# Decode attention with a 512-key window: more wo rows on the lowest five DMA engines, an alignment directive for three instruction streams, and another order of the last sums

## The chip, the cores and the metric

The kernel runs on one core of one Trainium2 chip. The metric is the device time of one execution in microseconds (us). The time of before is the median of 3 runs. One further execution was profiled; its page and trace are what is read here.

## The reference

One token of 32 sequences attends to the last 512 keys of a cache. There are 32 query heads and 8 key and value heads of width 128; `W` is 512.

```python
q = (x @ wq).reshape(B, Sq, Hq, Dh).transpose(0, 2, 1, 3)        # 32 x 32 x 1 x 128
k = jnp.repeat(k_cache[:, :, Sk - W:, :], rep, axis=1)           # rep = 4
v = jnp.repeat(v_cache[:, :, Sk - W:, :], rep, axis=1)
scores = jnp.einsum("bhqd,bhkd->bhqk", q, k) * (Dh ** -0.5)
p = _softmax(scores, axis=-1)
o = jnp.einsum("bhqk,bhkd->bhqd", p, v)
return o.transpose(0, 2, 1, 3).reshape(B, Sq, Hq * Dh) @ wo      # wo: 4096 x 512
```

The inputs are bf16: `x` 32 x 512, `wq` 512 x 4096, `wo` 4096 x 512, and two caches of which 32 MB each are read. With `wq` and `wo` of 4 MB each that makes 75.5 MB.

## The kernel before

The batch is cut into eight groups `q` of four sequences. For each group the keys (4 MB) and the values (4 MB) are loaded into one of two buffers each, `K_sb[q % 2]` and `V_sb[q % 2]`, with 128 partitions of 32 KB. `wq` is loaded first, into `V_sb[1]`, and `wo` last, into `K_sb[0]`. The SyncE engine (SP) issues all of these loads in the order of the list `LOADS`: `K0 K1 V0.0 K2 V1.0 ... V7.0 V7.1 A0 A1 A2 A3 W0 W1 W2`. A load waits for the buffer it overwrites. ACT issues the three small loads of `x` at the very start.

What each engine does is written out by hand in the lists `PE_OPS`, `DVE_OPS` and `ACT_OPS`; the function `needs` gives the semaphores that an operation waits for. The letters, for a group q:

- `Tq.w`: DVE transposes half `w` of the keys from `K_sb` into `KT_sb[:, w]` (L491). `Sq.w`: the scores of that half on PE (L353). `M`: maximum (DVE). `X`: exponential (ACT). `N`: division by the sum (DVE).
- `E`: PE moves the probabilities into the layout of the values by 16 matmuls with selection matrices from `E_sb` (L368). `G`: ACT copies them from PSUM. `B`: DVE and ACT spread them into `bd` (L511, L552).
- `Pq.g0.g1`: probabilities times values on PE, 4 matmuls for each of 32 groups of rows (L383). `C`: DVE and ACT pick the diagonal blocks into `C_sb` (L516, L557).
- `F` and `H`: PE folds `C_sb` by head (L395) and the extra rows of each head (L404). `D` and `U`: ACT copies these into `o_sel` (L561) and `o_ext` (L566).

A head has 128 rows of `wo`. `NI` = 30: the first 4 x 30 rows lie on 4 partitions of `K_sb[0]`, 30 rows on each, loaded in three pieces `W0`, `W1`, `W2` of 20, 8 and 2 rows (`WOP`). The last `NX` = 8 rows of each head ("extra rows") lie on 32 partitions of `wx_row`, a view of `QT_sb[0:64]`, one head on each. They are loaded by `A0` to `A3` (L262), which `HEADS` cuts into 20, 5, 5 and 2 heads:

```python
HEADS = [(0, 20, 4, 0), (20, 25, 1, 32), (25, 30, 1, 33), (30, 32, 1, 34)]
```

`wx_row` is first set to zero by ACT (operation `Z0`, L572), since not all of its 64 partitions are written; `A0` waits for that.

The last sum into `Y_ps`, over heads and rows, goes as follows: PE waits for `D7`, then for W0 (80 matmuls, L421), then for `U7` and the extra rows (32 matmuls, L435), then for W1 (32) and W2 (8). The four quarters of the output columns lie on four groups of PSUM partitions; DVE (L524) and ACT (L582) each copy half, and SP and ACT store them.

POOL makes the selection matrices: `E_sb` holds, for each of 4 values of `k` and 4 of `e`, 128 columns that are zero but for every fourth (a memset, L297, and four copies, L301). It then builds the block diagonal queries `QBD` (L312) for each group. PE's instruction stream begins with `pe.addr_align(256, offset=178)` (L320), a directive that places the next instruction at slot 178 of a block of 256 instruction slots, here by no-ops.

Of the kernel before, what the change touches and what calls it, by code (L numbers as in the profile page):

```python
# [5 lines left out]
BF16 = mybir.dt.bfloat16  # L6
F32 = mybir.dt.float32
ACTF = mybir.ActivationFunctionType
# [10 lines left out]
PE_OPS = """  # L19
S0.0 S0.1 S1.0 S1.1 E0 E1 P0.0.32 S2.0 F0 H0 S2.1 P1.0.12 E2 P1.12.32 F1 H1 S3.0 S3.1 P2.0.12 E3  # L20
P2.12.32 F2 H2 S4.0 S4.1 P3.0.12 E4 P3.12.32 S5.0 S5.1 S6.0 P4.0.4 E5 P4.4.8 S6.1 P4.8.24 E6 P4.24.32
F3 H3 S7.0 P5.0.20 S7.1 P5.20.32 E7 F4 H4 P6.0.32 F5 H5 P7.0.32 F6 H6 F7 H7
"""
DVE_OPS = """
T0.0 T0.1 T1.0 M0 T1.1 N0 M1 N1 B0.0.4 B1.0.4 T2.0 T2.1 M2 N2 B2.0.4 T3.0 T3.1 M3 N3 B3.0.4 T4.0
# [2 lines left out]
"""  # L28
ACT_OPS = """
X0 X1 G0 B0.4.8 G1 B1.4.8 C0.0.4 D0 U0 X2 G2 B2.4.8 C1.0.4 D1 U1 X3 G3 B3.4.8 C2.0.4 D2 U2 X4 G4 B4.4.8  # L30
C3.0.2 X5 G5 B5.4.8 X6 G6 C4.0.2 B6.4.7 D3 U3 B6.7.8 Z0 X7 C5.0.2 G7 B7.5.6 D4 U4 B7.6.8 C6.0.2 D5 U5 C7.0.2
D6 U6 D7 U7
"""

LOADS = """
# [2 lines left out]

X_PARTS = [(0, 25), (25, 30), (30, 32)]
V_PIECES = 5 * [[0, 32]] + 2 * [[0, 16, 32]] + [[0, 18, 32]]  # L40
WOP = [(0, 20), (20, 28), (28, 30)]
HEADS = [(0, 20, 4, 0), (20, 25, 1, 32), (25, 30, 1, 33), (30, 32, 1, 34)]


# [4 lines left out]
def bass_standalone__sliding_block_cached__sampling_kernel(  # L49
# [8 lines left out]
    B, Sq, D = x.shape  # L58
    _, HKV, SK, DH = k_cache.shape
    HD = wq.shape[1]  # L60
    HQ = HD // DH
    REP = HQ // HKV
    W = min(4096, max(256, SK // 4))
    assert (B, Sq, D, HKV, SK, DH, HQ, REP, W) == (32, 1, 512, 8, 2048, 128, 32, 4, 512)
    P = 128
    DKT = D // P
    SCALE = float(DH) ** -0.5
    NQ = B // 4
    KB = 4
    R = W // KB  # L70
    NI = 30
    NX = DH - 4 * NI
    NG = 4

# [2 lines left out]
    ends, total = {}, {}  # L77
# [52 lines left out]
    with ExitStack() as es:  # L130
# [15 lines left out]
        o_sel = sb("o_sel", [P, NI, B], BF16)  # L146
        o_ext = sb("o_ext", [64, NX, B], BF16)
        F_ext = sb("F_ext", [P, 64], F32)
        E_sb = sb("E_sb", [P, KB, REP, 32, KB], BF16)
        F_sb = sb("F_sb", [P, 4, HQ, 4], F32)  # L150
        mask = sb("mask", [P, HKV], F32)
        maxv = sb("maxv", [P, NQ], F32)
# [4 lines left out]

        wq_sb = V_sb[1][:, :].rearrange("p (kt n) -> p kt n", kt=DKT)
        wo_sb = K_sb[0][:, 0:NI * D].rearrange("p (i n) -> p i n", i=NI)
        wx_row = QT_sb[0:64].rearrange("p j w h t -> p (j w h t)")  # L160
        wx_sb = wx_row.rearrange("p (i n) -> p i n", i=NX)


# [15 lines left out]
        def folds(q):  # L179
# [8 lines left out]
        sem_out = sem("sem_out")  # L188
        names = (
            "pe_xT pe_q pe_Y dve_xT dve_q dve_QT dve_m dve_r dve_c act_q act_warm out_y "  # L190
            "pool_x pool_e pool_ei pool_q pool_f pool_m pool_j pool_qbd pool_fz"
        ).split()
        s = {n: sem(n) for n in names}
        op_sem = {key: sem("op_%s_%s" % key) for key in total}
# [1 line left out]
        def v_waits(q, g0, g1):  # L196

            for i, g in enumerate(V_PIECES[q][:-1]):
                if g0 <= g < g1:
                    c = sum(1 for p in range(q % 2, q + 1, 2) if len(V_PIECES[p]) > i + 1)  # L200
                    yield g, sem_v[q % 2][i], 16 * c

        for b0, b1 in X_PARTS:
            nc.scalar.dma_start(
# [33 lines left out]
        @block.sync  # L238
        def _(sp):
            wait = Waits(sp)  # L240
            wo_h = wo.rearrange("(h r) n -> h (r n)", r=DH)
            wo_r = wo_h[:, 0:4 * NI * D].rearrange("h (d m) -> h d m", d=4)
            for op in ops_of(" ".join(LOADS)):
                kind, q = op[0], op[1]
                if kind == "K":
                    if q >= 2:
                        wait([ends["T", q - 2, 1]])
                    sp.dma_start(K_sb[q % 2][:, :], rows(k_cache, q)).then_inc(sem_k[q % 2], 16)
                elif kind == "V":
                    if q == 1:  # L250
                        sp.wait_ge(s["pe_q"], 8)
                    r0, r1 = (4 * g for g in V_PIECES[q][op[2]:op[2] + 2])
                    if q >= 2:
                        wait([ends["P", q - 2, r1 // 4 - 1]])
                    sp.dma_start(  # L255
                        V_sb[q % 2][:, r0 * DH:r1 * DH], rows(v_cache, q, r0, r1)
                    ).then_inc(sem_v[q % 2][op[2]], 16)
                elif kind == "A":
                    wait([ends["Z", 0]])
                    h0, h1, k, p0 = HEADS[q]  # L260
                    n = (h1 - h0) // k
                    sp.dma_start(  # L262
                        wx_row[p0:p0 + 4 * n:1 if k == 4 else 4, :],
                        wo_h[h0:h1, 4 * NI * D:].rearrange("(k j) m -> j k m", k=k),
                    ).then_inc(sem_wx, 16)
                else:
                    wait([ends["T", NQ - 2, 1]])
                    i0, i1 = WOP[q]
                    sp.dma_start(  # L269
                        wo_sb[:, i0:i1, :].rearrange("p i n -> p (i n)"),  # L270
                        wo_r[:, :, i0 * D:i1 * D],
                    ).then_inc(sem_wo[q], 16)
            store(sp, 0)

        @block.gpsimd
        def _(pool):
            wait = Waits(pool)

            def diag(t, pattern, name):
# [14 lines left out]

            diag(E_id[:, :, :].rearrange("p e (b h) -> p e b h", b=4),
                 [[-1, REP], [-4, 4], [-16, HKV]], "pool_ei")
            pool.memset(E_sb[:, :, :, :, :], 0.0).then_inc(s["pool_e"], 1)  # L297
            pool.wait_ge(s["pool_e"], 1)
            pool.wait_ge(s["pool_ei"], 2)
            for k in range(KB):  # L300
                pool.tensor_copy(E_sb[:, k, :, :, k], E_id[:, :, :]).then_inc(s["pool_e"], 1)  # L301
            pool.wait_ge(s["pool_e"], 5)
            pool.wait_ge(s["pool_q"], 1)
            pool.wait_ge(s["dve_QT"], 1)
            for q in range(NQ):
                if q >= 2:
                    wait([ends["S", q - 2, 1]])
                for b in range(4):
                    pr = slice(32 * b, 32 * b + 32)
                    if q or b:  # L310
                        pool.wait_ge(s["pool_qbd"], 4 * q + b)
                    pool.tensor_copy(  # L312
                        QBD[pr, q % 2].rearrange("p (w t) (h c) -> p w t h c", w=2, h=HKV)[
                            :, :, :, :, 4 * b:4 * b + 4],
                        QT_sb[pr, q].rearrange("p w (h e) t -> p w t h e", h=HKV),
                    ).then_inc(s["pool_qbd"], 1)

        @block.tensor
        def _(pe):
            pe.addr_align(256, offset=178)  # L320
            wait = Waits(pe)
            pe.wait_ge(s["pool_x"], 2)
            pe.wait_ge(sem_x, 16 * len(X_PARTS))
# [38 lines left out]

            def to_value_rows(q):
                if q == 0:
                    pe.wait_ge(s["pool_e"], 5)
                for e in range(REP):
                    for k in range(KB):
                        ins = pe.matmul(  # L368
                            EP_ps[:, e * R:(e + 1) * R],
                            lhsT=E_sb[:, k, e].rearrange("p m j -> p (m j)"),  # L370
                            rhs=P_bf[:, k * R:(k + 1) * R],
                            start=k == 0, stop=k == KB - 1, tile_position=(0, 0),
                        )
                return ins
# [35 lines left out]
            for op in orders["PE"]:  # L410
                wait(needs(op))
                run[op[0]](*op[1:]).then_inc(op_sem["PE", op[0]], 1)
            wait([ends["D", NQ - 1]])
            for j, (i0, i1) in enumerate(WOP):
                pe.wait_ge(sem_wo[j], 16)
                last = j == len(WOP) - 1
                for cs in ((0, 1), (2, 3)) if last else (range(4),):
                    for i in range(i0, i1):
                        for c in cs:
                            n = 2 * (c % 2) + c // 2  # L420
                            ins = pe.matmul(  # L421
                                Y_ps[32 * c:32 * (c + 1), 0:P],
                                lhsT=o_sel[:, i, :],
                                rhs=wo_sb[:, i, n * P:(n + 1) * P],
                                start=i == 0, stop=i == NI - 1, tile_position=(0, 32 * c),
                            )
                    if last:
                        ins.then_inc(s["pe_Y"], 1)
                if j == 0:
                    wait([ends["U", NQ - 1]])  # L430
                    pe.wait_ge(sem_wx, 16 * len(HEADS))
                    for i in range(NX):
                        for c in range(4):
                            n = 2 * (c % 2) + c // 2
                            pe.matmul(  # L435
                                Y_ps[32 * c:32 * (c + 1), 0:P],
                                lhsT=o_ext[:, i, :],
                                rhs=wx_sb[:, i, n * P:(n + 1) * P],
                                start=False, stop=False, tile_position=(0, 32 * c),
                            )  # L440

        def spread_args(q, h):
            return bd[:, q % 2, :, h, :], PTc[:, q % NG], mask[:, h:h + 1]
# [83 lines left out]
        def _(act):  # L527
# [39 lines left out]
                    o_ext[:, :, 4 * q:4 * q + 4],  # L567
                    EP_ps[0:64, 0:4 * NX].rearrange("p (b i) -> p i b", b=4), ACTF.Copy)

            def zero(_):  # L570
                act.wait_ge(s["pool_qbd"], 4 * NQ)
                return act.activation(  # L572
                    wx_row, junk[0:64, 0:1].to_broadcast([64, NX * D]), ACTF.Copy
                )

            run = {"X": exponential, "G": gather, "B": spread, "C": pick, "D": folded,
                   "U": folded_ext, "Z": zero}
            for op in orders["ACT"]:
                wait(needs(op))
                run[op[0]](*op[1:]).then_inc(op_sem["ACT", op[0]], 1)  # L580
# [34 lines left out]
```

## Time and profile before

| | us |
|---|---|
| median of 3 runs (lowest, highest) | 184.43 (184.24, 184.46) |
| profiled execution | 184.59 |
| its span | 183.3 |
| PE busy, share of the span | 120.4, 66% |
| DVE busy | 106.7, 58% |
| ACT busy | 54.2, 30% |
| POOL busy | 17.1, 9% |
| HBM read over the span | 75.53 MB, 412 GB/s |

The page divides the span into 40 slices and gives, for each, the busy tenths of an engine and the mean share of the 16 DMA engines. Its DMA part gives queues: q1 has the loads that SP issues, q10 the ones of ACT, and the queues of kind "instruction" (q8 and q14) fetch the engines' own instructions. The chain of waits follows the program back from its last instruction. The timeline lists instructions by start time, with the idle time before and what ended it.

### The profile page before, as it was taken

To read this page: it belongs to the slowest core of one execution; us is meant where nothing else is said; L and a number is where in the kernel's file an instruction comes from. 1 tells how busy PE (TensorE), PEld (TensorE's weight loads), DVE (VectorE), ACT (ScalarE), POOL (GpSimd) and SP (SyncE) were. 2 spreads that over 40 slices of the span, in tenths; PEclk is the share of its full clock that TensorE was granted. 3 is DMA by queue.
4 is the path that set the end of the run, shared out by engine and by line. 5 is a ranking of instruction groups with operands and counts; after the bars stand their busy time and mean duration, and the time that the engine had idled before them with its cause. 6 is when DMAs were issued, how large, how long until landed. Compare 5 with 4: busy or idle time off the path is not lost.

```text
span 183.3 us, 3870 instructions
## 1 busy us (share of the span) xinstructions
PE 120.4 (66%) x1676; PEld 58.0 (32%) x1676; DVE 106.7 (58%) x109; ACT 54.2 (30%) x101; POOL 17.1 (9%) x53
## 2 busy tenths in 40 slices
PE   0029802416779699429944995440799978999984
PEld 0013300002535344304520252000255433655463
DVE  0042399998569534973289326999825994703030
ACT  3001300010590527501650135001053693803040
POOL 7900013020200020002000200001000000000000
PEclk9999995555769999996995599655559999999999
DMA  6998999989999999999999999999999999999981
GB/s 234 459 443 386 429 458 454 422 386 451 458 443 383 429 454 447 415 401 451 442 429 415 424 442 440 408 429 451 436 408 404 426 426 429 432 418 427 436 359 62
DMA packets 3517, 75.80 MB, mean 414 GB/s; under 512 B 429, under 2 KB 525, under 8 KB 653
## 3 DMA queue, kind: packets, MB, share of 16 engines
q1 hardware_dynamic: 3409, 75.52, 96.5%
q8 instruction: 13, 0.21, 0.5%
q10 hardware_dynamic: 92, 0.05, 0.1%
q14 instruction: 3, 0.02, 0.0%
HBM read 75.53 MB, written 0.03 MB: 412 GB/s over the span
## 4 chain that ended last, share of the span: by engine, by line
DMA 65%; DVE 19%; PE 8%; issue 4%; SPq 3%; ACT 0%; DVEq 0%
DMA K_sb<-in_k_cache_dram 32%; DVE KT_sb L491 16%; DMA V_sb<-in_v_cache_dram 16%; DMA K_sb<-in_wo_dram 11%; DMA V_sb<-in_wq_dram 7%; PE ps L336 5%; PE ps L383 2%; DVE QT_sb L483 2%; SPq L262 2%; SPq L255 1%; PE ps L421 1%; PE ps L353 1%; DVE C_sb L516 0%; SPq L269 0%; ACT KT_sb L533 0%
## 5 line engine op out<-in xcount | busy, mean ns | idle before, releaser
L491 DVE STREAM_TRANSPOSE KT_sb<-K_sb 128x4096 f32<-128x4096 f32 x16 | 70.5, 4430 | 7.2 <-DMA K_sb<-in_k_cache_dram 7.1
L383 PE MATMUL ps<-V_sb,bd 32*128 32x512 bf16 x1024 | 64.0, 402 | 4.4 <-DMA V_sb<-in_v_cache_dram 2.1
L353 PE MATMUL ps<-KT_sb,QBD 128*32 128x512 bf16 x256 | 24.7, 522 | 35.2 <-DVE KT_sb L491 26.0
L383 PEld LDWEIGHTS ps<-V_sb,bd 32*128 32x128 bf16 x1024 | 27.7, 98 | 37.8 <-issue 14.1
L353 PEld LDWEIGHTS ps<-KT_sb,QBD 128*32 128x32 bf16 x256 | 6.4, 111 | 50.4 <-DVE KT_sb L491 31.3
L539 ACT ACTIVATE P_f<-ps,negmax 128x512 f32<-128x512 f32 x8 | 5.5, 687 | 56.8 <-DVE negmax L499 56.8
L557 ACT ACTIVATE C_sb<-ps 32x512 f32<-32x512 f32 x22 | 12.9, 588 | 24.4 <-PE ps L383 24.2
L552 ACT ACTIVATE bd<-PTc,mask 128x512 bf16<-128x512 bf16 x31 | 20.1, 712 | 0.3
L312 POOL COPY QBD<-QT_sb 32x128 bf16<-32x128 bf16 x32 | 9.3, 289 | 106.3 <-PE ps L353 87.2
L511 DVE TENSOR_SCALAR bd<-PTc,mask 128x512 bf16<-128x512 bf16 x33 | 9.4, 349 | 14.0 <-ACT PTc L546 14.0
L516 DVE COPY C_sb<-ps 32x512 f32<-32x512 f32 x10 | 6.9, 693 | 13.9 <-PE ps L383 13.8
L395 PE MATMUL ps<-C_sb,F_sb 128*128 128x120 f32 x64 | 9.2, 286 | 6.8 <-ACT C_sb L557 6.5
L497 DVE TENSOR_REDUCE maxv<-ps 128x1 f32<-128x512 f32 x8 | 5.5, 687 | 10.8 <-PE ps L353 10.7
L395 PEld LDWEIGHTS ps<-C_sb,F_sb 128*128 128x128 f32 x64 | 7.7, 191 | 9.6 <-ACT C_sb L557 8.4
L368 PE MATMUL ps<-P_bf,E_sb 128*128 128x128 bf16 x128 | 9.9, 239 | 1.0 <-DVE P_bf L505 1.0
L336 PE MATMUL ps<-V_sb,bd 128*128 128x512 bf16 x32 | 9.0, 451 | 2.0 <-DMA V_sb<-in_wq_dram 2.0
L546 ACT ACTIVATE PTc<-ps 128x512 bf16<-128x512 f32 x8 | 4.7, 593 | 18.3 <-PE ps L368 18.3
L368 PEld LDWEIGHTS ps<-P_bf,E_sb 128*128 128x128 bf16 x128 | 8.4, 108 | 4.9 <-DVE P_bf L505 2.8
L325 PE MATMUL ps<-bd 32*128 32x128 bf16 x4 | 0.6, 298 | 10.5 <-DMA bd<-in_x_dram 10.5
L533 ACT ACTIVATE KT_sb<-ps 128x512 bf16<-128x512 f32 x4 | 2.4, 597 | 17.0 <-PE ps L336 17.0
L453 DVE CAST bd<-ps 128x512 bf16<-128x512 f32 x1 | 0.7, 692 | 11.2 <-PE ps L325 11.2
L480 DVE CAST KT_sb<-ps 128x512 bf16<-128x512 f32 x4 | 2.8, 692 | 6.0 <-PE ps L336 6.0
(37 smaller groups left out, 44.1 us busy)
## 6 DMA issues: line engine op xcount, KB each, us to landing
K_sb<-in_k_cache_dram SPq DMA_DIRECT2D x8, 4096.0 KB, 24.6
V_sb<-in_v_cache_dram SPq DMA_DIRECT2D x5, 4096.0 KB, 28.7
V_sb<-in_v_cache_dram SPq DMA_DIRECT2D x4, 2048.0 KB, 20.6
V_sb<-in_wq_dram SPq DMA_DIRECT2D x1, 4096.0 KB, 12.3
K_sb<-in_wo_dram SPq DMA_DIRECT2D x1, 2560.0 KB, 17.6
V_sb<-in_v_cache_dram SPq DMA_DIRECT2D x1, 2304.0 KB, 14.2
V_sb<-in_v_cache_dram SPq DMA_DIRECT2D x1, 1792.0 KB, 14.9
K_sb<-in_wo_dram SPq DMA_DIRECT2D x1, 1024.0 KB, 19.4
```

Source lines behind the costliest of these rows:

```text
L312: pool.tensor_copy(QBD[pr, q % 2].rearrange("p (w t) (h c) -> p w t h c", w=2, h=HKV)[:, :, :, :, 4 * b:4 * b + 4], QT_sb[pr, q].rearrange ...
L336: ins = pe.matmul(ps[:, n], lhsT=xT_sb[:, kt, :], rhs=wq_sb[:, kt, n * 512:(n + 1) * 512], start=kt == 0, stop=kt == DKT - 1, tile_positio ...
L353: ins = pe.matmul(S_ps[32 * c:32 * c + 32, :], lhsT=QBD[:, q % 2, 2 * w + t, c0:c0 + 32], rhs=KT_sb[:, w, :, KB * h:KB * h + KB, t], start ...
L368: ins = pe.matmul(EP_ps[:, e * R:(e + 1) * R], lhsT=E_sb[:, k, e].rearrange("p m j -> p (m j)"), rhs=P_bf[:, k * R:(k + 1) * R], start=k = ...
L383: ins = pe.matmul(O_ps[:, b, :], lhsT=bd[pr, q % 2, 4 * g:4 * g + 4].rearrange("p r h e -> p (r h e)"), rhs=V_sb[q % 2][pr, 512 * g:512 * ...
L395: ins = pe.matmul(folds(q), lhsT=F_sb[:, d].rearrange("p h d -> p (h d)"), rhs=C_sb[:, q % 2, :, NI * d:NI * d + NI], start=d == 0, stop=d ...
L491: return dve.transpose(KT_sb[:, w].bitcast(F32).rearrange("p r c t -> p r (c t)"), K_sb[q % 2][:, :].bitcast(F32).rearrange("p (r w c) -> ...
L497: dve.tensor_reduce(maxv[:, q:q + 1], S_ps, AX.X, ALU.max).then_inc(s["dve_m"], 1)
L511: ins = dve.tensor_scalar(o, i, m, None, op0=ALU.mult)
L516: ins = dve.tensor_copy(*pick_args(q, r))
L552: ins = act.activation(o, i, ACTF.Copy, scale=m)
L557: ins = act.activation(*pick_args(q, r), ACTF.Copy)
```

## The change

- `NI` becomes 29 and `NX` 12: W0 has 19 rows per partition instead of 20, and each of the 32 extra-row partitions has 12 rows (12 KB) instead of 8.
- `wx_row` becomes a view of `KT_sb[0:64, 0]`. It is set to zero by POOL, after the scores `S7.0`, instead of by ACT.
- At the start of the DVE, ACT and POOL streams, ahead of the loads of `x`, stands `addr_align(128, offset=0, max_nops=0)`: the next instruction lies at slot 0 of a block of 128 slots, and the padding is branched over. PE's offset becomes 154.
- `E_sb` holds one strip of 132 columns for each `e` instead of four matrices of 128, and the matmul takes a window of 128 columns that starts at column 3, 2, 1 or 0. POOL fills it by a smaller memset and one copy.
- In the last sum the extra rows come first: PE waits for `U7` and the extra rows (48 matmuls), then for `D7` and W0 (76), W1 (32) and W2 (8). `H7` stands ahead of `F7`, and `U6 U7` ahead of `D6 D7`.

```diff
-F3 H3 S7.0 P5.0.20 S7.1 P5.20.32 E7 F4 H4 P6.0.32 F5 H5 P7.0.32 F6 H6 F7 H7
+F3 H3 S7.0 P5.0.20 S7.1 P5.20.32 E7 F4 H4 P6.0.32 F5 H5 P7.0.32 F6 H6 H7 F7
...
-C3.0.2 X5 G5 B5.4.8 X6 G6 C4.0.2 B6.4.7 D3 U3 B6.7.8 Z0 X7 C5.0.2 G7 B7.5.6 D4 U4 B7.6.8 C6.0.2 D5 U5 C7.0.2
-D6 U6 D7 U7
+C3.0.2 X5 G5 B5.4.8 X6 G6 C4.0.2 B6.4.7 D3 U3 B6.7.8 X7 C5.0.2 G7 B7.5.6 D4 U4 B7.6.8 C6.0.2 D5 U5 C7.0.2
+U6 D6 U7 D7
...
-WOP = [(0, 20), (20, 28), (28, 30)]
+WOP = [(0, 19), (19, 27), (27, 29)]
...
-    NI = 30
+    NI = 29
     NX = DH - 4 * NI
...
-        E_sb = sb("E_sb", [P, KB, REP, 32, KB], BF16)
+        E_sb = sb("E_sb", [P, REP, 33, KB], BF16)
...
-        wx_row = QT_sb[0:64].rearrange("p j w h t -> p (j w h t)")
+        wx_row = KT_sb[0:64, 0].rearrange("p r c t -> p (r c t)")[:, 0:NX * D]
...
+        for eng in (nc.vector, nc.scalar, nc.gpsimd):
+            eng.addr_align(128, offset=0, max_nops=0)
+
         for b0, b1 in X_PARTS:
             nc.scalar.dma_start(
...
-                    wait([ends["Z", 0]])
+                    sp.wait_ge(s["pool_z"], 1)
...
-            pool.memset(E_sb[:, :, :, :, :], 0.0).then_inc(s["pool_e"], 1)
+            pool.memset(E_sb[:, :, :, :], 0.0).then_inc(s["pool_e"], 1)
...
-            for k in range(KB):
-                pool.tensor_copy(E_sb[:, k, :, :, k], E_id[:, :, :]).then_inc(s["pool_e"], 1)
-            pool.wait_ge(s["pool_e"], 5)
+            pool.tensor_copy(E_sb[:, :, 0:32, KB - 1], E_id[:, :, :]).then_inc(s["pool_e"], 1)
+            pool.wait_ge(s["pool_e"], 2)
...
+            wait([ends["S", NQ - 1, 0]])
+            pool.memset(wx_row, 0.0).then_inc(s["pool_z"], 1)
...
-            pe.addr_align(256, offset=178)
+            pe.addr_align(256, offset=154)
...
+                    window = E_sb[:, e].rearrange("p m j -> p (m j)")
                     for k in range(KB):
                         ins = pe.matmul(
                             EP_ps[:, e * R:(e + 1) * R],
-                            lhsT=E_sb[:, k, e].rearrange("p m j -> p (m j)"),
+                            lhsT=window[:, KB - 1 - k:KB - 1 - k + P],
...
+            wait([ends["U", NQ - 1]])
+            pe.wait_ge(sem_wx, 16 * len(HEADS))
...
+            for i in range(NX):
+                projected(o_ext[:, i, :], wx_sb[:, i], range(4), first=i == 0)
             wait([ends["D", NQ - 1]])
             for j, (i0, i1) in enumerate(WOP):
                 pe.wait_ge(sem_wo[j], 16)
                 last = j == len(WOP) - 1
                 for cs in ((0, 1), (2, 3)) if last else (range(4),):
                     for i in range(i0, i1):
-                        for c in cs:
...
+                        ins = projected(o_sel[:, i, :], wo_sb[:, i], cs, last=i == NI - 1)
                     if last:
                         ins.then_inc(s["pe_Y"], 1)
-                if j == 0:
-                    wait([ends["U", NQ - 1]])
-                    pe.wait_ge(sem_wx, 16 * len(HEADS))
...
-            def zero(_):
-                act.wait_ge(s["pool_qbd"], 4 * NQ)
-                return act.activation(
-                    wx_row, junk[0:64, 0:1].to_broadcast([64, NX * D]), ACTF.Copy
-                )
...
```

`projected` is a new function that holds the four matmuls of one row, the same as in the loops it replaces, with `start` on the first extra row and `stop` on the last row of W2.

More of the change, by code (lines that the diff above doesn't have):

```diff
@@ L190, in bass_standalone__sliding_block_cached__sampling_kernel @@
             "pe_xT pe_q pe_Y dve_xT dve_q dve_QT dve_m dve_r dve_c act_q act_warm out_y "
-            "pool_x pool_e pool_ei pool_q pool_f pool_m pool_j pool_qbd pool_fz"
+            "pool_x pool_e pool_ei pool_q pool_f pool_m pool_j pool_qbd pool_fz pool_z"
         ).split()
@@ L364, in to_value_rows @@
                 if q == 0:
-                    pe.wait_ge(s["pool_e"], 5)
+                    pe.wait_ge(s["pool_e"], 2)
                 for e in range(REP):
+                    window = E_sb[:, e].rearrange("p m j -> p (m j)")
                     for k in range(KB):
@@ L412, in _, with projected @@
                 run[op[0]](*op[1:]).then_inc(op_sem["PE", op[0]], 1)
+            wait([ends["U", NQ - 1]])
+            pe.wait_ge(sem_wx, 16 * len(HEADS))
+            def projected(lhsT, rhs, cs, first=False, last=False):
+                for c in cs:
+                    n = 2 * (c % 2) + c // 2
+                    ins = pe.matmul(
+                        Y_ps[32 * c:32 * (c + 1), 0:P],
+                        lhsT=lhsT, rhs=rhs[:, n * P:(n + 1) * P],
+                        start=first, stop=last, tile_position=(0, 32 * c),
+                    )
+                return ins
+            for i in range(NX):
+                projected(o_ext[:, i, :], wx_sb[:, i], range(4), first=i == 0)
             wait([ends["D", NQ - 1]])
@@ L418, in _ @@
                     for i in range(i0, i1):
-                        for c in cs:
[L420 to L425, printed above, removed]
-                            )
+                        ins = projected(o_sel[:, i, :], wo_sb[:, i], cs, last=i == NI - 1)
                     if last:
                         ins.then_inc(s["pe_Y"], 1)
-                if j == 0:
-                    wait([ends["U", NQ - 1]])
-                    pe.wait_ge(sem_wx, 16 * len(HEADS))
[L432 to L440, printed above, removed]
         def spread_args(q, h):
@@ L568, in folded_ext @@
                     EP_ps[0:64, 0:4 * NX].rearrange("p (b i) -> p i b", b=4), ACTF.Copy)
-            def zero(_):
-                act.wait_ge(s["pool_qbd"], 4 * NQ)
-                return act.activation(
-                    wx_row, junk[0:64, 0:1].to_broadcast([64, NX * D]), ACTF.Copy
-                )
             run = {"X": exponential, "G": gather, "B": spread, "C": pick, "D": folded,
-                   "U": folded_ext, "Z": zero}
+                   "U": folded_ext}
             for op in orders["ACT"]:
```

## The prediction, made before the changed kernel ran

> **What bounds it now.** I read the page's slices and DMA rows first, then the chain of waits, then the stretches and the timeline of the last ten microseconds, and last the trace's records of single DMA packets (start, length, bytes, queue) and of the landings.
>
> ```profile
> DMA  6998999989999999999999999999999999999981
> ...
> q1 hardware_dynamic: 3409, 75.52, 96.5%
> q8 instruction: 13, 0.21, 0.5%
> q10 hardware_dynamic: 92, 0.05, 0.1%
> q14 instruction: 3, 0.02, 0.0%
> ```
>
> The 16 DMA engines are full from the second slice to the last but one; the bytes set the time. Sixteen packets on q8 and q14 fetch instructions, on the same engines.
>
> ```profile
> 160.86 19.41 DMA K_sb<-in_wo_dram
> 180.27 0.04 issue
> 180.32 1.00 PE ps L421 x40
> 181.31 0.02 issue
> 181.34 0.27 ACT P_bf L582
> ```
>
> The chain ends through wo: W1 lands at 180.27, W2 at 180.90 (landing record), and the span ends at 183.3, 2.40 after W2.
>
> ```profile
> 172.00:177.80 5.80, 5.29 (x72) 3.34 (x60) 1.39 (x2) 1.93 (x6) 0.00 (x0) 1.00 0.93 391
> 177.80:180.30 2.50, 1.86 (x112) 1.61 (x112) 0.00 (x0) 0.01 (x1) 0.00 (x0) 1.00 0.54 211
> ```
>
> The column before the last is the DMA share: it falls to 0.54 in the last 2.5 us. Some engines are done while others still carry; the kernel waits for the last of them. So the sum is made per DMA engine. A DMA that uses 16 engines lands 16 times, so the steps between the landings of V7.1, W0 and W2 sort the engines. From V7.1 to W0 (8 packets of 20 KB, 0.76 each) eleven take 6.1, one of these 7.6; five take 8.0 or 8.3. The five carry the extra rows: A0 to A2 have 5 groups of rows and A3 has 2, so two engines get 7 rows of 8 KB and three get 6, at 0.31 a row.
>
> The fetches sort the rest. A 16 KB fetch on q8 takes 1.0 to 1.1, and the packet behind it 0.47 longer (1228 ns for 761 at 173.1): 1.56 in all. They go round eight engines that carry no extra rows; the twelve before 173 hit four of them twice, and the thirteenth (179.1) finds its engine done. The three 8 KB fetches on q14 (packets at 87.65, 100.83, 108.06) fall on three of the five: 0.32 each, and the next packet takes 1875, 1594 and 1566 ns for 1220, so 0.98, 0.69 and 0.67.
>
> ```
> W2 landings before (us), by engine            change   after
> 3: no fetch, no extra rows   177.41..177.76   -0.30    177.1..177.5
> 4: one 16 KB fetch           178.98..179.13   -0.30    178.7..178.8
> 4: two 16 KB fetches  180.47 .54 .58 180.90   -0.30    180.17 .24 .28 .60
> 7 rows, no 8 KB fetch        179.84           +0.76    180.60
> 7 rows, fetch at 100.8       180.31     -0.69 +0.76    180.38
> 6 rows, no 8 KB fetch        179.34           +0.61    179.95
> 6 rows, fetch at 108.1       179.95     -0.67 +0.61    179.89
> 6 rows, fetch at 87.6        180.45     -0.98 +0.61    180.08
> ```
>
> **The change, part by part.** *Rows.* W0 goes from 20 to 19 rows: 8 KB less per engine. From 20 KB in 0.761 and 8 KB in 0.309, 1 KB costs 0.0377, so -0.30. An extra row of 12 KB for 8 costs 0.151 more: +0.91 for six, +1.06 for seven, net +0.61 and +0.76.
>
> *Directive.* [...] The directive jumps to slot 0 of the next block, so the three fetches should start near 0.7, when ACT and SP issue their first loads; the first load packet starts at 1.80 (q1). A fetch done by then costs nothing; a fetch after it costs 0.67 to 0.98 as before. I take none: the columns -0.69, -0.67, -0.98 stand.
>
> But the streams are not equally long. Behind the directive ACT has some 118 instructions (eight X read their sum with one more) and POOL under 75. DVE has 129 up to its last copy, L525 of the changed kernel. So DVE enters a second block as soon as it has sent the last pick (L516 here, sent by 175.4), and fetches again. Before, the packet came 2.5 to 4.5 after the last instruction sent, about three load packets, so I expect it at 176.5 to 178.5, when that engine has W0 or W1 left. Price 0.67 to 0.98; I take 0.67, because the packets are the smallest there. If DVE's ring is that of the fetch at 87.6 (DVE sent its last at 85.2, and the other two fit ACT and POOL), the engine goes from 180.08 to 180.75. The last landing is then 180.75 instead of 180.90.
>
> *The directive's jump.* [...] x lands at 10.41 and L453 ends at 11.86, wq lands at 13.03: 1.1 of cover, and behind it K2 is sent at 35.4 while V0 lands only at 41.75. Some 5 us of delay would reach no transfer. I take 0. [...]
>
> *PE's offset.* [...] Cost 0. The 24 no-ops saved end before x lands: 0.
>
> *Zeroing.* Z0 leaves ACT (3.60 at 148.21); ACT's next X7 waits until 154.74 for negmax, so no gain. POOL's memset of 6144 columns takes 5.4 by the 1.80 of L289's 2048; S7.0 ends at 146.4, so it ends near 151.9, and SP comes to A0 at 157.10. Cover 5.2; behind it W0 is sent at 160.2 while engines drain V7.1 only at 168.2. Cost 0. DVE's T7.1 runs beside it; if POOL slows it, S7.1 waits until 152.7 for V5.1 anyway, 1.5 after T7.1.
>
> *E_sb.* POOL saves 1.3 of memset and 1.0 of copies, then idles 17.6 for QT: 0. The 128 weight loads of L368 (108 ns) now start at odd 2-byte places, which no row shows. Bounds: no loss (L325's strided ones take 88 ns) to another 108 each. I take 0, the row it is nearest to.
>
> *Order at the end.*
>
> ```profile
> 176.23 1.12 PE L395 MATMUL ps<-C_sb,F_sb 128*128 128x120 f32 x8 [0.29 <-DVE C_sb L516]
> 177.28 0.19 PEld L404 LDWEIGHTS ps<-C_sb,F_ext 128*64 128x64 f32 x2
> 177.96 1.30 PE L421 MATMUL ps<-K_sb,o_sel 128*32 128x128 bf16 x80 [0.38 <-DMA K_sb<-in_wo_dram]
> 179.19 0.63 PE L435 MATMUL ps<-QT_sb,o_ext 64*32 64x128 bf16 x32
> 180.32 0.93 PE L421 MATMUL ps<-K_sb,o_sel 128*32 128x128 bf16 x40 [0.49 <-DMA K_sb<-in_wo_dram]
> ```
>
> F7 and H7 in either order are sent by 177.5. Then 48 extra-row matmuls at 0.014 (0.45 for 32 loads) to 178.2, then 76 of W0 at 0.0154 (1.23 for 80) to 179.3. D7 is ready by about 177.9, during the extra rows. W1 now lands 0.63 before W2, at 180.1: PE has 0.8 to spare, and the tail behind W2 stays 2.40. What is queued behind the new waits on U7 and the extra rows is W0's matmuls only; the extra rows land near 172.4. Cost 0.
>
> **Sum.** 180.75 + 2.40 + 1.29 (184.59 of the profiled execution less its span) = 184.44, 0.15 under that execution. It was 0.16 above the median of 184.43, so 184.28. A measurement tells about 0.2%, 0.37 us, from no change; this is inside.
>
> **Rivals.** (a) No late fetch, or one that comes too late to matter. The last landing is 180.60, shared by a twice-fetched engine and a seven-row one: 184.13. For: DVE is over by one slot only. [...]
> (b) A larger gain: the two engines at 180.60 are last by their start (first load packets start from 1.80 to 2.73; without that 0.2 to 0.3 the four others end at 180.28 and seven rows at 180.4) and nothing is late: 183.93.
> (c) Slower: the three fetches come after 1.80, among the loads, and DVE pays twice: 180.08 + 0.67 + 0.67 = 181.42, so 184.95. It decides if the first q14 packet starts after its engine's first q1 packet. For: x, sent at 0.74, needed until 1.71 to start a packet. Against: an 8 KB fetch needs only 0.31 once started, and first packets take 1.2 to 2.1 anyway.
> (d) Slower: PE becomes the bound. If weight loads from odd places cost another 108 ns, the 16 of E7 add 1.7 to the chain E7, P6, P7, F7; with 0.8 of cover that is 0.9 over my sum, 185.2. It decides from 50 ns a load.
> (e) The directive does nothing: three fetches stay, the engine of 87.6 ends at 180.45 + 0.61 = 181.06, time 184.59.
>
> **Numbers.** Forecast 0.38 (0.03 faster, 0.31 same, 0.04 slower; own range 184.1 to 184.6); (a) 0.22 (0.09 faster, 0.13 same); (b) 0.14 faster; (c) 0.10 slower; (d) 0.08 slower; (e) 0.08 (0.06 same, 0.02 slower). Faster 0.26, same 0.50, slower 0.24. The range 183.9 to 184.95 takes in (a), (b), (e) and the near half of (c).
>
> **What would show it.** No q14 packet between 2 and 170 us, one near 177; three before 1.8. Of W2's landings the first three near 177.3, the last between 180.6 and 180.9, the extra-row engines risen by 0.6 to 0.8 less their fetch. PE idle before W1's matmuls, by about 0.8. I am wrong if PE is not idle there (d), if q14 packets stand among the loads (c, e), or if an engine with 7 rows ends past 181.

## The result, and the profile after

| | before | after |
|---|---|---|
| median (lowest, highest), us | 184.44 (184.24, 184.74), 6 runs | 187.66 (186.57, 188.23), 6 runs |
| profiled execution, its span, us | 184.59, 183.3 | 188.09, 186.7 |

The ratio over the runs is 1.0163, with an interval of 1.0128 to 1.0198. By the medians the changed kernel is slower by 3.2 us, beyond the range's upper end of 184.95. In the sections below, a time "against" another means the runs of that kernel against those of the kernel before on the same chip. Ratios and medians are over fast runs; one run, of experiment 11 (188.62), was slow as a whole and is left out.

The page of the changed kernel, slices and DMA queues:

```profile
DMA  6999999986999999999999999999999999999981
GB/s 230 444 446 422 435 407 428 449 348 218 449 414 407 418 449 449 425 446 421 407 425 442 442 439 425 414 421 442 442 435 390 428 428 425 420 436 417 427 368 62
...
q1 hardware_dynamic: 3409, 75.52, 95.1%
q8 instruction: 13, 0.21, 0.5%
q10 hardware_dynamic: 92, 0.05, 0.1%
q14 instruction: 4, 0.03, 0.1%
```

The packets on q1 and their bytes are the same as before. What is new is a dip in the ninth and tenth slice, at 37 to 47 us: 348 and 218 GB/s between neighbours of 449. The engines ran dry there. The stretch of 40 to 44 us shows it closer, in the kernel before and then in the changed one (the column before the last is the DMA share):

```profile
40.00:44.00 4.00, 1.90 (x16) 0.52 (x16) 3.97 (x3) 0.78 (x2) 0.00 (x0) 0.50 1.14 492
```

```profile
40.00:44.00 4.00, 1.57 (x20) 0.44 (x16) 4.00 (x2) 0.00 (x0) 0.00 (x0) 0.50 0.34 143
```

The timeline says which load was missing: K2, the next in the list; V1.0 is sent right behind it. Its SP issue, before and after:

```profile
35.36 0.54 SPq L248 DMA_DIRECT2D K_sb<-in_k_cache_dram  x1
```

```profile
42.91 0.54 SPq L251 DMA_DIRECT2D K_sb<-in_k_cache_dram  x1
```

K2 is sent 7.55 us later. From there the loads are late by a constant: K2's first landing is at 54.85 for 51.45 (+3.40), V7.1's at 171.64 for 168.22 (+3.42), the last of W2 at 184.33 for 180.90 (+3.43). So the whole loss lies ahead of 55 us, and the end of the kernel, to which nearly all of the prediction went, is only shifted. The chain of waits of the changed kernel leads back to its first microsecond:

```profile
0.77 0.42 issue
1.19 2.75 ACTq L207
3.94 0.04 issue
3.98 0.37 ACTq L207
4.35 0.03 issue
4.38 13.83 DMA bd<-in_x_dram
18.21 0.14 issue
18.35 0.60 PE ps L329 x4
...
163.38 20.32 DMA K_sb<-in_wo_dram
183.71 0.04 issue
183.75 0.99 PE ps L424 x40
184.74 0.02 issue
184.77 0.27 ACT P_bf L577
```

Here ACT's first send of x begins at 1.19 instead of 0.74, and takes 2.75 instead of 0.58. The jump itself, a branch at L204, stands just ahead at 0.74. x's first packet starts at 7.3 instead of 1.71, while wq's 32 KB packets run from 1.81 on; x lands at 18.21 instead of 10.41. PE's first matmuls start at 18.35 instead of 10.54. The projection, DVE's QT (L484) and the transposes T0 (L492) follow one after the other, and K2 overwrites the keys that T0 reads. The sum of the delay: the projection, which waited for wq before, starts at 19.72 instead of 13.17 (6.55 later), and its 32 matmuls take 10.03 instead of 9.02. That is how 7.8 us of x become 7.55 us of K2; why the projection itself took longer is not shown.

### The profile page after: what moved, and what is told of

Read it like the earlier page. It is cut to its first block, busy times and chain, and to the rows that moved or that the text cites. A ratio compares the mean times of both kernels' runs of the same rounds, so it can differ in the third digit from the quotient of the medians.

```text
span 186.7 us, 3870 instructions
## 1 busy us (share of the span) xinstructions
PE 119.9 (64%) x1688; PEld 58.9 (32%) x1688; DVE 107.0 (57%) x109; ACT 50.8 (27%) x100; POOL 20.1 (11%) x51
## 4 chain that ended last, share of the span: by engine, by line
DMA 44%; PE 21%; DVE 19%; issue 9%; SPq 2%; ACT 2%; ACTq 2%; DVEq 0%
DMA K_sb<-in_k_cache_dram 25%; DVE KT_sb L492 14%; DMA K_sb<-in_wo_dram 11%; PE ps L388 10%; DMA bd<-in_x_dram 7%; PE ps L340 5%; PE ps L373 2%; PE ps L357 2%; DVE QT_sb L484 2%; ACTq L207 2%; SPq L265 2%; ACT C_sb L558 1%; DVE C_sb L517 1%; PE ps L400 1%; DVE bd L512 1%
## 5 line engine op out<-in xcount | busy, mean ns | idle before, releaser
L492 DVE STREAM_TRANSPOSE KT_sb<-K_sb 128x4096 f32<-128x4096 f32 x16 | 70.5, 4430 | 6.0 <-DMA K_sb<-in_k_cache_dram 5.8
L388 PE MATMUL ps<-V_sb,bd 32*128 32x512 bf16 x1024 | 61.6, 389 | 4.3 <-DMA V_sb<-in_v_cache_dram 2.3
L388 PEld LDWEIGHTS ps<-V_sb,bd 32*128 32x128 bf16 x1024 | 27.0, 95 | 36.0 <-issue 10.8
L400 PE MATMUL ps<-C_sb,F_sb 128*128 128x116 f32 x64 | 10.0, 303 | 6.5 <-ACT C_sb L558 6.5
L400 PEld LDWEIGHTS ps<-C_sb,F_sb 128*128 128x128 f32 x64 | 8.6, 208 | 9.3 <-ACT C_sb L558 8.0
L340 PE MATMUL ps<-V_sb,bd 128*128 128x512 bf16 x32 | 10.0, 490 | 0.8 <-DVE bd L454 0.8
L320 POOL MEMSET KT_sb<- 64x6144 bf16 x1 | 5.2, 5210 | 21.8 <-PE ps L357 21.8
```

The costliest lines, as they stand in the source:

```text
L340: ins = pe.matmul(ps[:, n], lhsT=xT_sb[:, kt, :], rhs=wq_sb[:, kt, n * 512:(n + 1) * 512], start=kt == 0, stop=kt == DKT - 1, tile_positio ...
L388: ins = pe.matmul(O_ps[:, b, :], lhsT=bd[pr, q % 2, 4 * g:4 * g + 4].rearrange("p r h e -> p (r h e)"), rhs=V_sb[q % 2][pr, 512 * g:512 * ...
L400: ins = pe.matmul(folds(q), lhsT=F_sb[:, d].rearrange("p h d -> p (h d)"), rhs=C_sb[:, q % 2, :, NI * d:NI * d + NI], start=d == 0, stop=d ...
L492: return dve.transpose(KT_sb[:, w].bitcast(F32).rearrange("p r c t -> p r (c t)"), K_sb[q % 2][:, :].bitcast(F32).rearrange("p (r w c) -> ...
```

## The experiments

**1. The changed kernel without the directive.**

```diff
-        for eng in (nc.vector, nc.scalar, nc.gpsimd):
-            eng.addr_align(128, offset=0, max_nops=0)
```

> The changed kernel without the directive at the head of the DVE, ACT and POOL streams; all else as changed. Theory J (the jump makes ACT send x late, x lands at 18.2 instead of 10.4, K2 is sent at 42.9 after the DMA engines have run dry at about 41.3): without the jump x lands near 10.4, K2 is sent near 35.4, no hole between 40 and 48 us, the three 8 KB fetches are back near 88, 101 and 108, and the time is 184.3 to 184.7. Rival R (the moved rows, the zeroing on POOL, the shifted weight windows or the new order at the end cost it): the time stays at 186.6 or more and x still lands early.

Measured: 185.00 against 184.48, ratio 1.0027 (1.0017 to 1.0037). x lands at 10.37, K2 is sent at 34.91, the stretch of 40 to 44 is full (1.12). So 2.7 of the 3.2 us hang on those three lines. The time missed the expected 184.7 by 0.3: the other edits bring a small loss, not nothing. The three q14 packets are back at 88.7, 101.0 and 108.2; one hits an engine with seven 12 KB rows, which lands last, at 181.25. That is the case of rival (e), which priced it at 181.06 on an engine with six.

**2. The kernel before with the directive alone.** The same three lines ahead of the loads of x.

> The kernel before with the directive alone, in the same place ahead of the x loads. Theory J: x lands near 18, DMA share in 40 to 44 us about 0.4, time 186.6 to 188.3. Rival R: x may land late, but the time is 184.2 to 184.8.

Measured: 187.38 against 184.48, ratio 1.0161 (1.0124 to 1.0198), within noise the ratio of the whole change. K2 is sent at 42.33, and the share falls:

```profile
40.00:44.00 4.00, 1.64 (x16) 0.45 (x16) 4.00 (x2) 0.00 (x0) 0.00 (x0) 0.50 0.67 229
```

The directive alone suffices.

**3. The loads of x ahead of ACT's jump.** In the changed kernel, DVE and POOL jump as before, ACT jumps once it has sent x.

```diff
-        for eng in (nc.vector, nc.scalar, nc.gpsimd):
+        for eng in (nc.vector, nc.gpsimd):
             eng.addr_align(128, offset=0, max_nops=0)
         for b0, b1 in X_PARTS:
...
+        nc.scalar.addr_align(128, offset=0, max_nops=0)
```

> The changed kernel with ACT's directive moved behind the three x loads; DVE and POOL jump as before. Theory J: x lands near 10.4, K2 near 35.4, no hole; the late 8 KB fetch of DVE stays, near 171 us, and its engine ends the loads; time 184.2 to 184.6. Rival F (the fetch packets that the jumps bring at 1.8 to 4.2 us hold x back, not the late send): DVE and POOL still fetch there, x lands at 14 or later, time 186 or more.

Measured: 185.67, ratio 1.0065 (1.005 to 1.008). x is sent at 0.74 again and lands at 11.20, K2 is sent at 36.65, the share at 40 to 44 is 1.08: the hole is gone and 2 us with it. The expected 184.2 to 184.6 was missed by 1. The last landing, 181.90, is on an engine with six extra rows and the late DVE fetch (q14 at 170.63; 9.55 from V7.1 to W0, where six rows alone take 8.57). That engine already lands V7.1 at 169.28, 1.1 behind the earliest of its kind, 168.21. It seems to have paid for an early fetch and then for the late one. This is the kind of rival (c), early and late fetch on one engine, priced at 181.42.

**4. x later, without a jump.** In the kernel before, ACT waits for POOL's first instruction, and no stream jumps.

```diff
+        nc.scalar.wait_ge(s["pool_x"], 1)
         for b0, b1 in X_PARTS:
```

> The kernel before with one wait ahead of the x loads on ACT: POOL's first memset (ends near 0.93), so that x is sent some 0.3 us later; no directive and no jump. Theory J in its narrow form (a send 0.3 to 0.45 us later is enough, because x's packets then stand behind the first load packets of 32 KB): x's first packet starts after 5, x lands at 15 or later, time 186 or more. Rival F: x lands near 11, time 184.3 to 184.6, since no fetch is moved.

Measured: 184.73, ratio 1.0026 (1.0002 to 1.0051). x is sent at 0.96 and its first send takes the usual 0.57; it starts its first packet at 3.53 and lands at 14.2; K2 is sent at 38.16. The profiled execution has no hole (share 1.05). So 0.22 us of delay in the send cost 3.8 us in the landing, and 2.8 us on K2 are still covered. The packet records show why the landing moves so much. Before, 25 of the 32 packets of x (1 KB each) start by 2.19, ahead of the bulk of wq. Here none starts before 3.53, and then they come in fives, 1.25 apart, about the length of one 32 KB packet (1.22): x takes turns with the big packets. The expected 186 and more were missed: this delay is too small to decide.

**5. x later still.** The same with the count 2 in place of 1.

> The kernel before with x sent after POOL has made xsel (its second instruction ends near 1.47), so some 0.75 later than before; no directive, no jump, no fetch moved. Theory J (a late send alone makes the hole): with 0.22 later x landed at 14.2 and K2 went out at 38.2, with 0.45 later at 18.2 and 42.9; with 0.75 x lands at 17 to 20, K2 goes out after 41.5, the DMA share in 40 to 44 us falls under 0.7 and the time is 186 to 188.5. Rival F (the jump itself or its fetches are needed for the hole): no hole, time 184.3 to 185.

Measured: 186.12 against 184.59, ratio 1.0081 (1.0058 to 1.0105). x is sent at 1.50 (0.56 long) and lands at 16.66.

```profile
40.00:44.00 4.00, 1.74 (x16) 0.31 (x8) 4.00 (x1) 0.00 (x0) 1.15 (x4) 0.50 0.87 336
```

```profile
39.81 0.54 SPq L249 DMA_DIRECT2D K_sb<-in_k_cache_dram  x1
```

The first line is the stretch of 40 to 44 us, the second is from the timeline. Now the hole is there, K2's sixteen landings are 0.74 (the first, 52.19) to 1.4 later (the last, 54.36 for 52.97), the last of W2 comes at 182.73 (+1.83), and no stream has jumped. A late x makes the hole by itself. The time is at the lower end of the expected 186 to 188.5; x landed a little ahead of the expected 17, and the share stayed above the expected 0.7.

**6. ACT's jump alone, and 7. the jumps of DVE and POOL alone**, both in the kernel before.

```diff
+        for eng in (nc.scalar,):                 # 6;  (nc.vector, nc.gpsimd) in 7
+            eng.addr_align(128, offset=0, max_nops=0)
```

> The kernel before with the directive on ACT alone, ahead of the x loads. Open is why ACT's first x send took 2.75 to 3.05 us behind the jump, for 0.58 before. Theory A (ACT's own jump, through its own fetch): the send takes 2.5 or more, x lands near 18, K2 goes out after 42, time 186.6 to 188.3. Rival B (the three fetches of three engines together slow it): the send takes under 1 us, x lands at 16 to 17, K2 goes out near 40, time 185 to 186.6.

> The kernel before with the directive on DVE and POOL alone. Theory A: x is sent as before and lands near 10.4, no hole; the rows are the old ones, so the engine of DVE's fetch (180.5 before) pays early and late, up to 181.0 to 181.5, and the time is 184.5 to 185.2. Rival B: the fetches of DVE and POOL slow ACT's send as well, x lands at 14 or later, time above 185.5.

Measured: ACT alone 187.43 against 184.50, ratio 1.0143 (1.0102 to 1.0184); DVE and POOL alone 185.14, ratio 1.0034 (1.002 to 1.0048). The first microseconds of the timeline with ACT's jump alone, and its stretch:

```profile
0.74 0.42 SPq L211 DMA_DIRECT2D V_sb<-in_wq_dram  x1
...
1.18 3.72 ACTq L207 DMA_DIRECT2D bd<-in_x_dram  x3
```

```profile
40.00:44.00 4.00, 1.57 (x20) 0.44 (x16) 4.00 (x2) 0.00 (x0) 0.00 (x0) 0.50 0.33 139
```

The jump puts the loads of x behind wq (0.74) and stretches the three sends from 1.19 (in the kernel before) to 3.72. With the other two jumps x is sent at 0.74, lands at 10.48, and there is no hole; the loss of 0.6 is at the end (last W2 181.35, a late q14 at 171.48). So the rival that the fetches of DVE and POOL, or their traffic, hold up x is out: it is ACT's own jump.

**8. No late fetch.** Experiment 3, with DVE's four copies into `F_ext` moved to ACT, so that DVE has 125 instructions behind its jump up to the last copy instead of 129.

```diff
-                dve.tensor_copy(
+                act.activation(
                     F_ext[:, p0:p0 + 4 * n].rearrange("p (j k) -> p k j", k=4)[:, 0:k],
-                    F_hd[:, h0:h1].rearrange("p (k j) -> p k j", k=k),
+                    F_hd[:, h0:h1].rearrange("p (k j) -> p k j", k=k), ACTF.Copy,
                 ).then_inc(s["dve_c"], 1)
```

> The changed kernel with ACT's directive behind the x loads, and the four copies into F_ext done by ACT instead of DVE, so that DVE's stream behind its directive stays under 128 slots. Theory: no 8 KB fetch after 5 us; the last landing of W2 is that of a twice-fetched engine or a seven-row engine, 0.30 before that of the kernel before; time 184.0 to 184.25, that is faster by 0.1 to 0.25%. Rival (the late fetch costs nothing, or the moved rows cost more than 0.3): 184.3 to 184.7, the same as with ACT's directive moved alone.

Measured: 185.06 against 184.39, ratio 1.0035 (1.0021 to 1.0048). No q14 packet among the last loads; the last of W2 is at 181.03 for 181.90 in experiment 3, so the late fetch is worth some 0.87. The expected 184.0 to 184.25 was missed by 0.8: here all three fetches are at the front and x is on time, and the kernel is no faster than experiment 1 without the directive (185.00). Three lines of the DMA view, stretches of 1.7 to 8 us in this kernel, then of 160 to 175 in experiment 3 and 170 to 180 in the changed kernel:

```profile
q14 instruction: 3, 0.02, 1.6%
```

```profile
q14 instruction: 1, 0.01, 0.1%
```

```profile
q14 instruction: 1, 0.01, 0.2%
```

The early packets start at 1.74, 3.9 and 6.1, while the loads run from 1.8. They are seen at once in wq, whose sixteen landings span 12.39 to 13.74, for 12.58 to 13.03 in the kernel before. The five engines with extra rows land V7.1 at 168.03, 168.62, 168.64, 168.84 and 169.37; in the kernel before, with its fetches in the middle, at 168.26, 168.47, 168.86, 168.97 and 169.41. So the fetches that ran among the first loads took about as much of the load time as those in the middle.

**9. The old rows without the directive.** Experiment 1 with `NI = 30`, the old `WOP` and PE's offset of 178; POOL's zeroing, the strips of `E_sb` and the new order of the last sum stay.

> The changed kernel without the directive, and with the old split of rows (NI 30, 8 extra rows, PE's offset 178); what stays of the change is the zeroing on POOL, the smaller E_sb with its windows, and the new order at the end. Theory: these three cost nothing, time 184.3 to 184.6, ratio within 0.1% of before; then the 0.27% that the change costs without its directive is the moved rows on engines that still have their 8 KB fetch. Rival: the order, the windows or POOL cost it, time 184.8 to 185.1.

Measured: 184.65 against 184.59, ratio 0.9999 (0.999 to 1.0008), last W2 at 180.79. These three parts cost nothing that can be told from noise, as the prediction had them. Experiment 1's loss is therefore that of the rows (or of the offset that goes with them).

**10. x sent by SP, ahead of wq**, in the changed kernel (`nc.sync.dma_start` in place of `nc.scalar.dma_start` for the three parts).

> The changed kernel with the x loads issued by SP, ahead of wq; SP has no directive, so all three jumps stay where they are and x does not wait for one. Theory J: x lands before 5, the matmuls of wq start when wq lands (some 1 us later than before, since SP sends it third), no hole, time 184.2 to 184.8. Rival F: the 8 KB fetches at 1.8 to 4.2 still delay the start and K2 is sent after 41, time 186 or more.

Measured: 185.76 against 184.39, ratio 1.0071 (1.0058 to 1.0083); expected were 184.2 to 184.8. x lands at 3.74 and there is no hole, but wq is sent at 1.78, a full microsecond later, and V7.1's first landing is 169.12 for 168.22. The delay of the first big load is paid nearly in full (0.90 for a send 1.04 later). The late fetch comes on top (last W2 181.78).

This run also shows what experiment 8 did not: fetches in the front that end ahead of the loads. The stretch of 1.5 to 2.7 us:

```profile
q1 hardware_dynamic: 42, 0.03, 11.7%
q14 instruction: 3, 0.02, 5.6%
```

The three fetches start at 1.73, 2.00 and 2.10 and are over by 2.41; only x's small packets run beside them, and wq's first 32 KB packet starts at 2.76. Here the fetches leave no trace: wq's landings span 13.48 to 13.95, as narrow as before, and the five engines with extra rows land V7.1 within 0.34 of each other (169.12 to 169.46), for 1.34 in experiment 8. Less the 0.90 by which all loads are late, the last W2 is at 180.88, for 180.75 in the prediction.

**11. PE's offset 0 in the kernel before.**

> The kernel before with PE's stream placed at slot 0 of a block instead of 178, so that each of its fetches comes 178 slots later: the twelfth at about matmul 33 of W0 (178.5) instead of in P7 (172), the thirteenth not at all. If the last landing of W2 is that of the engine that the fetch at 172 falls on, it goes from 180.9 to at most 180.6 and the time to 184.0 to 184.25. The 191 no-ops (113 took 8.2 us before) end near 14.6, so PE starts some 4 us later and K2 goes out near 39.5, still ahead of the point where the engines run dry. Rival (the fetch still lands on a busy engine and costs the same, or the later start reaches a transfer): 184.4 or more.

Measured: 186.51 against 184.59, ratio 1.0115 (1.0084 to 1.0146); expected were 184.0 to 184.25. No fetch left the loads: packets still lie at 171.8 and 179.0, and a fourteenth comes behind the loads' end. So the offset did not move them as expected; what sets their places is not shown. The last W2 lands at 180.79, where it did, so the DMA engines are not what costs. The chain of waits shows a gap in PE in the middle of the last matmuls:

```profile
180.21 0.29 PE ps L421 x8
180.50 0.66 issue
181.16 0.70 PE ps L421 x32
```

PE waits there for nothing that the trace names, and no q8 packet starts in the gap; its cause is not shown. It accounts for about half of what this execution lost (185.79 for 184.59): the other 0.65 lies outside the span. K2 is sent at 38.50 here, 3.14 later than before, and its first landing (51.35) is not late. The run is no test of the change's own offset of 154, whose chain has no such gap (`x40` in one piece above).

## Why the prediction was wrong, step by step

**The directive's jump: this step failed.** It was taken as 0, since "Some 5 us of delay would reach no transfer". By experiment 2 the term is 2.9 us (187.38 for 184.48). Both halves of the argument were off. The cover is smaller: K2 sent 2.80 late (experiment 4) or 3.14 late (11) makes no hole in the profiled execution, 4.45 late (5) makes K2 land 0.74 to 1.4 later, 7.55 late (the change) 3.40. So the cover is some 3 to 4 us. And the delay is larger: the prediction gave a late send no size, and what counts is not the send but the landing:

```
                    send starts  takes  x lands   K2 sent   share 40-44
before                 0.74       0.58   10.41     35.36       1.14
4: POOL's first        0.96       0.57   14.2      38.16       1.05
5: POOL's second       1.50       0.56   16.66     39.81       0.87
2: directive alone     1.18       3.05   18.47     42.33       0.67
6: ACT's jump alone    1.18       3.09   19.43     42.87       0.33
after                  1.19       2.75   18.21     42.91       0.34
```

The rise is steepest at the front: wq is sent at 0.74 as well, and a small load that is sent 0.22 behind it already loses 3.8 us. The row that would have told was at hand, and was used for something else in rival (c): x, sent at 0.74, lands at 10.41 although it is 32 KB. Most of its packets had gone out ahead of wq's; the last seven started only between 6.16 and 8.81. That row said what happens to a packet of x that comes behind wq. None of the rivals (a) to (e) had x late.

The traces show a delay behind the jump: ACT's first send starts 0.45 us later (1.19 for 0.74) and takes some 2.2 to 2.5 longer (2.75 to 3.09 for 0.58). What makes it is not shown, and the prediction never put a size on it.

**The directive does what it says, but it is no gain.** The three fetches come at the front, as predicted, at 1.765, 1.802 and 3.771: not all "before 1.8". "A fetch done by then costs nothing" did not get its condition: by experiment 8 they cost their engines about what the middle ones did, so with x on time the columns of -0.69, -0.67 and -0.98 were not to be had (in the changed kernel itself the hole hides these fetches, see below). The sentence itself holds: in experiment 10, where the fetches are over before wq's first packet, they cost nothing that can be seen, and the last landing is as predicted to 0.13, once the 0.90 of the later wq is taken off. No run has both, early fetches at no cost and wq on time.

**The late DVE fetch: right in place, low in price.** It came at 174.0 in a kernel that runs 3.4 late, so 6 to 8 us sooner than the predicted 176.5 to 178.5; in experiment 3 it came at 170.6. It did fall on an engine with six extra rows, which lands last. The lower end of 0.67 was taken with the smallest packets as the reason; it measured 0.97 (9.54 from V7.1 to W0 beside 8.57), the upper end. That it comes at all was the author's estimate from DVE's 129 instructions behind the jump, and the runs bear it out: in experiment 8, with 125, no q14 packet starts from 100 to 183. Where between the two counts the limit lies is not shown.

**Rows: right.** W0 takes 5.80 for 6.10 (-0.30 predicted, -0.30 measured), six rows 8.57 for 7.98 (+0.61, +0.59), seven 9.05 for 8.28 (+0.76, +0.77). The landings of W2 in the changed kernel, less the shift of 3.42, against the predicted:

```
                             after           less 3.42        predicted
3: nothing extra             180.65..180.93  177.23..177.51   177.1..177.5
4: one 16 KB fetch           182.15..182.35  178.73..178.93   178.7..178.8
4: two 16 KB fetches         182.70..184.01  179.28..180.59   180.17..180.60
five with extra rows         183.28..184.33  179.86..180.91   179.89..180.75
```

The engine at 182.70 is the odd one: it lands much like one with a single fetch. The packet records fit this: the first q8 fetch starts at 41.35, just as the loads run out, and K2's landings lie within 0.65 of each other (54.85 to 55.50), where before one engine was 1.1 behind (52.97). So the hole seems to have hidden that fetch, and with it what the early q14 fetches cost: wq lands from 12.62 to 13.85, but V7.1, on the five engines with extra rows, within 0.29 (171.64 to 171.93). The last landing, 184.33, would have been 184.01 without the late fetch. So even with x on time the rows had little to give: what the twice-fetched engines gain, the engines with 12 KB rows lose, above all where a fetch meets seven of them (experiment 1: 181.25).

**PE's offset: not shown on its own.** It was taken as 0, and no run shows that term, since none changes 178 to 154 alone. In the changed kernel the twelfth and thirteenth q8 packets start at 176.44 and 183.44, less the shift of 3.42 at 173.02 and 180.02, for 172.00 and 179.12 before. Experiment 1, with 154 and the new rows, loses 0.5 (185.00 for 184.48), experiment 9, with 178 and the old rows, nothing (184.65 for 184.59).

**Weight loads from odd places, zeroing, order: right at 0.** The groups of the changed kernel:

```profile
L373 PEld LDWEIGHTS ps<-P_bf,E_sb 128*128 128x128 bf16 x128 | 8.6, 110 | 4.9 <-DVE P_bf L506 3.2
...
L320 POOL MEMSET KT_sb<- 64x6144 bf16 x1 | 5.2, 5210 | 21.8 <-PE ps L357 21.8
```

A load takes 110 ns for 108, which ends rival (d), and the memset takes 5.2 for the 5.4 expected. At the end of the timeline PE waits for the last loads, but less than the 0.8 expected:

```profile
180.11 0.29 PE L409 MATMUL ps<-C_sb,F_ext 128*64 128x48 f32 x2 [0.38 <-ACT o_ext L567]
...
182.18 1.25 PE L424 MATMUL ps<-K_sb,o_sel 128*32 128x128 bf16 x76
183.75 0.93 PE L424 MATMUL ps<-K_sb,o_sel 128*32 128x128 bf16 x40 [0.32 <-DMA K_sb<-in_wo_dram]
```

H7 now waits 0.38 for ACT's U6, a wait the prediction did not have; it stays under cover. From W2 to the end it is 2.37 for 2.40. In experiment 1, without the hole, PE's wait for W1 is 0.95.

**What stays open.** Why ACT's first send behind its jump takes 2.75 to 3.1 us is not settled. It is ACT's own jump (experiments 6 and 7), yet the one early q14 packet of experiment 6 runs from 1.78 to 2.96, and the send from 1.18 to 4.27: they do not end together. Which fetch falls on which single engine was read from groups of landings only. And since two of the ten runs of experiment 4 lie at 185.87 and 186.65, its K2 may be at the edge of the cover.

## What to carry to other kernels

Before anything is put ahead of a kernel's first sends, follow the smallest load in that place to its landing and to the first buffer that its chain frees: price the landing, not the send, and measure the cover by what is sent last, here K2. The fetches that were moved to the front of the same full engines still took their time from the loads where the loads started there too (experiment 8: fetches from 1.74, loads from 1.8, wq's landings span 1.35 for 0.46 before); they cost nothing that can be seen only where they ended before the loads' first 32 KB packet (experiment 10: over by 2.41, that packet at 2.76, wq's landings span 0.47). And when nine tenths of a prediction are spent on the end of the trace, ask once what the edit at the very start would cost if its zero were wrong.

## What the runs showed that had not been expected

- The 32 KB load of 1 KB packets, sent 0.22 us behind a 4 MB one of 32 KB packets, landed 3.8 us later than when sent with it (experiment 4: 14.2 for 10.41), and 6.3 us later when sent 0.76 behind (experiment 5: 16.66).
- With a taken branch just ahead of it, ACT's first send started 0.45 us later (1.19 for 0.74) and took 2.75 to 3.1 instead of 0.58 (the changed kernel, experiments 2 and 6). Where ACT jumps (the changed kernel, experiments 2, 3 and 6), SP's second send of keys, at 1.9, also takes about 1.2 instead of 0.63, even in experiment 3, where ACT sends x ahead of its jump; in experiment 8, with the same jumps as 3, it takes 0.83.
- The late 8 KB instruction fetch cost the DMA engine it used 0.87 us (experiment 3 beside 8: 181.90 for 181.03) to 0.97 us of load time (the changed kernel: 9.54 for 8.57); the early ones cost about as much among the first loads as in mid-kernel (experiment 8: the five engines land V7.1 at 168.03 to 169.37, for 168.26 to 169.41 before), and nothing that can be seen ahead of the first big packet (experiment 10).
- With PE's offset at 0 and nothing else changed, a gap of 0.66 us stands among the last matmuls although the last load lands on time (experiment 11); its cause is open.
